# Attention into a token mixer on one core: the third and fourth head group's q and k are transposed in the whole array, and copied out one by one

## The chip, the cores and the metric

The kernel runs on one core of one Trainium2 chip. Its time is the device time in microseconds (us) of one execution; the median of three runs before the change is 184.26 us (183.81 to 184.72). A profile of one execution stands beside these runs. Its engines are TensorE (PE, with its weight loads as PEld), VectorE (DVE), ScalarE (ACT), GpSimd (POOL) and SyncE (SP), whose queue issues most of the transfers.

## The reference

Two steps, in float32, with q, k and v of shape (8 batches, 12 heads, 448 rows, 64 columns):

```
scores = q @ k^T / sqrt(64) - log(448)
x      = sigmoid(scores) @ v             # heads side by side: (8, 448, 768)
W      = (x @ w_q) @ (x @ w_k)^T / sqrt(64)
out    = max(W @ x, 0) @ w_out           # (8, 448, 768)
```

## The kernel before, in words

**The work and its letters.** Four heads of one batch make a head group; there are 24 groups, numbered n = 0 to 23, three to a batch. One letter of the string PLAN (lines 138 to 152) stands for one step, and the loop at line 828 walks through the string once and records the instructions of each step. So PLAN fixes the order of work on every engine; nothing is reordered later. The letters that matter here:

- S: one seventh of a group's scores (`scores`, line 311): four 64x64-tiled matmuls into a pair of PSUM banks, then one sigmoid on ACT over both banks (line 332) into an `at` tile. There are 168 of these, counted from S0. The first seven belong to group 0, S7 to S13 to group 1, S14 to S20 to group 2, and so on.
- P: one seventh of a group's `at @ v` (`values`, line 339): four matmuls into a bank pair that is held for all seven; after the seventh a copy (line 356) takes the result to `xt`.
- q, k (and a, b; and c, d, r, s): bring q or k of a group into the transposed layout `qk` that the scores read (`tr`, line 257). For q and k the transposes are matmuls with an identity, 28 in 64x64 tiles, four of them at a time in the four quarters of the array (`transposes`, line 231). For a and b they are 7 matmuls of 128x128 (`transposes_whole`, line 241). For c, d, r and s POOL and DVE do it without PE.
- 1: the next of the casts that DVE does (the others are POOL's); there are four of them, those marked with a dot in ORDER: q1, v0, k2, v23.
- O: a quarter or half of an output block; D: issue one output store that is ready.

**PSUM.** The eight banks of 2 KB are handed out by hand: each character of BANKS (line 66) is the next answer to "which bank": a digit 0 to 3 names a pair, a letter a to h a single bank (a and b make pair 0, g and h pair 3). A pair or bank that is named again waits for the copy or sigmoid that last read it.

**The four transposes of the change.** Groups 2 and 3 use the letters q and k before. For group 2, q's 28 transposes take pair 0, one S stands between, then k's 28 go into the same pair, and one DVE copy (line 301, 1792 columns) takes both out; the pair is held all the while. Group 3 does the same in pair 3. Which products those are: every matmul and transpose that PE is given has a number, from 0, in the order of the program; the list `products` holds them (3618 before). PE runs them in that order.

**Loads.** q, k and v of a group are float32 loads of 448 KB through SP's queue in the order ORDER (line 703), into a ring of six buffers; a load goes out when the cast of the tile that lay in its buffer is done. POOL casts to bf16 (lines 212 and 222), and rearranges some (lines 167 to 173).

**Two tables of waits on SP.** BEHIND (line 710) says for the last loads at which product they are put into SP's queue and behind which product the transfer has to start: q of group 23 at 2280, behind 2280; v of group 23 at 2816, behind 2530. HELD (line 521) does the same for three output stores of batch 5, behind products 3040, 3168 and 3168. SP is a queue: what stands behind a waiting transfer waits too.

Of the kernel before, what the change touches and what calls it, by code (L numbers as in the profile page):

```python
# [17 lines left out]
def kernel(  # L18
# [29 lines left out]
    def pool(name, bufs, **kw):  # L48
# [15 lines left out]
    pairs = [banks[:, 2 * n : 2 * n + 2] for n in range(4)]  # L64
    pairs16 = [banks16[:, 2 * n : 2 * n + 2] for n in range(4)]
    BANKS = (
        "abcd0123200233111020302312031203101031021g2012020120h1g21320"
        "132123103103213012302g01h20h1g2031a32102312g12h1201321gh0210"
        "12h01210321g201321g2h01gh201g20132cd302c302302131e301230ef31"
        "0ef3102102c302d320d320123cd20gh120g102310g102hg102312gh10210"  # L70
        "ef130210ef1302120120320312321031021021321a310320321320120123"
        "020210320120c3210210312"
    )
    given = list("".join(BANKS))
    held = set()
# [54 lines left out]
    def xt(u, j):  # L130
# [5 lines left out]


    PLAN = (
        "SSFKESSES1EEqESDD1DESjPPppSpDpPDSSSqS1kSpPPSqSpSkSDPPSPSxSxr"
        "sSWwDDDDSSwzDPpSPppSpPSrSwSwWsSPpXSPNpSpPPSUSqSzMSSkpSpPpSMS"  # L140
        "ppPSSxSxMScPpSdPSpppSSPwWwrWSSXWDWSSosOSNPpPSpppzPSSOOSxSrPP"
        "ppSUSsppzPSoSOSoSoSppMpSPPPPSSWOWWWScSdxWODSMDWSOSxCOSMppScP"
# [375 lines left out]

    opened = []
    stores, o_tiles = [], [0]  # L520
    HELD = {(5, 1, 1): 3040, (5, 2, 0): 3168, (5, 2, 1): 3168}

    def flush(n=None):

# [45 lines left out]
    def out_pair(act, tail):  # L570
# [36 lines left out]
        def store():  # L607
            for x in range(2):
                cols = slice(x * NB, (x + 1) * NB)
                if len(us) == 1:  # L610
                    behind_product(
                        (nc.scalar if ends and x else nc.sync).dma_start(
                            out=out[2 * w + us[0]].rearrange("(p i) d -> p i d", i=NI)[:, k : k + 5 : 4, cols], in_=o[HALF[x]],
                        ), HELD.get((2 * w + us[0], k, x), 0),
                    )
# [6 lines left out]

        stores.append((o_tiles[0] - 1, max(HELD.get((2 * w + us[0], k, x), 0) for x in range(2)), store))
        if tail or late:
# [74 lines left out]
    for _ in range(31):  # L699
# [2 lines left out]

    ORDER = (
# [5 lines left out]
    )  # L709
    BEHIND = {("q", 23): (2280, 2280), ("v", 23): (2816, 2530)}  # L710
    BY = {"s": [], "v": []}
    for x in ORDER.split():
        if x[0] == ".":
# [10 lines left out]
    def pump_loads():  # L724
        while len(loaded) < len(ORDER):
            nm, n = ORDER[len(loaded)]
            if len(ring) >= 6 and ring[-6] not in cast:
                break
            emit, m = BEHIND.get((nm, n), (0, 0))
            if emit >= len(products):  # L730
# [204 lines left out]
```

## Time and profile before

| what | value |
|---|---|
| median of three runs | 184.26 us (183.81 to 184.72) |
| the profiled execution's own time | 184.71 us |
| its span, first to last instruction | 182.8 us |
| granted TensorE clock | 0.994 |
| PE busy | 170.4 us (93%) |
| ACT busy | 159.4 us (87%) |
| DVE busy | 134.3 us (73%) |
| POOL busy | 116.8 us (64%) |

The 1.9 us between span and time lie around the program. Busy times are sums over the whole span, and the stages differ: a share says little on what a stage waits for. In the timeline's rows the engine's start and length in us come first, then engine, line, operation and shape; a bracket at the end says how long the engine sat idle before and what ended it. A PE row's length runs to the modelled end of its last matmul, so rows overlap: the distance between starts is what PE took.

### The profile page before, as it was taken

What the parts mean: (1) busy time and instruction counts of PE and PEld (TensorE: products, weight loads), DVE (VectorE), ACT (ScalarE), POOL (GpSimd) and SP (SyncE); (2) the same over time, 40 slices, a digit from 0 to 9 for tenths busy, and PEclk for the clock granted to TensorE, in tenths of its full rate; (3) what the DMA queues carried; (4) which work ended last, traced back from release to release, by engine and by line L of the source; (5) the groups of instructions that cost most, each with busy time, mean ns of one, the idle gap of its engine ahead of it and who ended that gap; (6) DMA issues with size and microseconds to landing.
All of it is one profiled execution on the core that took longest, in us unless ns stands there. A gap on an engine that the chain in (4) does not pass through costs nothing.

```text
span 182.8 us, 8404 instructions
## 1 busy us (share of the span) xinstructions
PE 170.4 (93%) x3617; PEld 112.8 (62%) x3618; DVE 134.3 (73%) x205; ACT 159.4 (87%) x207; POOL 116.8 (64%) x156
## 2 busy tenths in 40 slices
PE   7887789899999999999999999999999999999980
PEld 7644435545564555565556556556788798899960
DVE  2545699988998898988858887689786885694220
ACT  4699999999999999999998999899989979966230
POOL 1336886999589999699999927999999500000000
PEclk9999999999999999999999999999999999999997
DMA  5999999969999677999999999997589343433775
GB/s 174 371 382 274 329 382 398 364 212 279 351 402 331 219 295 207 353 285 349 396 232 327 349 307 292 359 359 250 193 255 252 106 96 87 95 90 93 176 181 164
DMA packets 24261, 48.51 MB, mean 265 GB/s; under 512 B 3872, under 2 KB 16416, under 8 KB 24224
## 3 DMA queue, kind: packets, MB, share of 16 engines
q1 hardware_dynamic: 24000, 47.69, 79.4%
q8 instruction: 28, 0.46, 1.0%
q10 hardware_dynamic: 224, 0.30, 0.7%
q14 instruction: 9, 0.07, 0.1%
HBM read 35.78 MB, written 11.01 MB: 256 GB/s over the span
## 4 chain that ended last, share of the span: by engine, by line
PE 76%; ACT 12%; DMA 3%; POOL 3%; issue 2%; DVE 1%; POOLq 0%; ACTq 0%
PE banks L121 72%; ACT at L332 12%; PE banks L124 4%; DMA ld<-in_v_dram 3%; POOL v L222 1%; POOL qk L212 1%; POOL qk L173 1%; POOL wout L755 0%; DVE xn L385 0%; ACT qk L806 0%; DVE ld L558 0%; ACT ld L558 0%; DVE zeros L691 0%; DVE zeros L690 0%; POOLq L222 0%
## 5 line engine op out<-in xcount | busy, mean ns | idle before, releaser
L332 ACT ACTIVATE at<-banks 128x896 bf16<-128x896 f32 x168 | 141.1, 943 | 5.4 <-PE banks L121 4.8
L121 PE MATMUL banks<-wout,mx 64*64 64x384 bf16 (+2 forms) x816 | 65.4, 324 | 0.0
L121 PE MATMUL banks<-qk 64*64 64x448 bf16 x672 | 60.7, 360 | 3.8 <-ACT at L332 3.0
L212 POOL CAST qk<-ld 128x896 bf16<-128x896 f32 x38 | 44.7, 1191 | 8.2 <-issue 5.6
L121 PEld LDWEIGHTS <-mx 64*64 64x64 bf16 (+2 forms) x816 | 39.2, 105 | 16.2 <-issue 6.0
L121 PE MATMUL banks<-at,v 64*64 64x448 bf16 x672 | 46.5, 350 | 0.8 <-ACT at L332 0.4
L121 PEld LDWEIGHTS <-qk 64*64 64x64 bf16 x672 | 26.5, 105 | 24.8 <-issue 17.8
L356 DVE CAST xt<-banks 128x896 bf16<-128x896 f32 x23 | 25.0, 1086 | 7.6 <-PE banks L121 5.7
L121 PEld LDWEIGHTS <-v 64*64 64x64 bf16 x672 | 22.9, 106 | 6.8 <-issue 1.7
L470 DVE TENSOR_SCALAR mx<-banks 128x896 bf16<-128x896 f32 (+1 forms) x21 | 19.9, 956 | 4.9 <-PE banks L121 4.2
L222 POOL CAST v<-ld 128x896 bf16<-128x896 f32 x22 | 20.3, 930 | 2.9 <-DMA ld<-in_v_dram 2.7
L272 DVE STREAM_TRANSPOSE qk<-qk 128x448 f32<-128x448 f32 x26 | 16.0, 630 | 0.1
L385 DVE COPY xn<-banks 128x896 bf16<-128x896 bf16 x21 | 13.1, 624 | 3.6 <-PE banks L124 2.6
L252 DVE STREAM_TRANSPOSE qk<-qk 32x448 f32<-32x448 f32 x24 | 15.3, 636 | 0.6
L170 POOL COPY qk<-qk 32x448 uint32<-32x448 uint32 x26 | 14.4, 554 | 1.6
L173 POOL COPY qk<-swap 32x448 uint32<-32x448 uint32 x26 | 14.4, 554 | 1.5
L121 PE MATMUL banks<-xt,wqk 64*64 64x448 bf16 (+1 forms) x84 | 13.8, 353 | 0.2 <-ACT at L332 0.2
L651 DVE COPY o<-banks 128x384 f32<-128x384 f32 x17 | 9.4, 554 | 3.4 <-PE banks L121 3.0
L124 PEld LDWEIGHTS <-xt 64*64 64x64 bf16 (+1 forms) x588 | 9.8, 108 | 3.0 <-issue 1.5
L124 PE MATMUL banks<-ident,xt 64*64 64x64 bf16 (+1 forms) x588 | 10.4, 194 | 0.2
L121 PE MATMUL banks<-wqk,tmp 64*64 64x448 bf16 (+3 forms) x72 | 8.5, 291 | 0.0
L121 PE MATMUL banks<-wq,tmp 64*64 64x448 bf16 (+2 forms) x72 | 8.4, 292 | 0.0
(67 smaller groups left out, 135.3 us busy)
## 6 DMA issues: line engine op xcount, KB each, us to landing
ld<-in_q_dram SPq DMA_DIRECT2D x24, 448.0 KB, 6.2
ld<-in_v_dram SPq DMA_DIRECT2D x24, 448.0 KB, 5.9
ld<-in_k_dram SPq DMA_DIRECT2D x23, 448.0 KB, 5.9
out_dram<-o SPq DMA_DIRECT2D x38, 192.0 KB, 4.7
out_dram<-ld SPq DMA_DIRECT2D x14, 192.0 KB, 2.8
ld<-in_moe_w_out_dram SPq DMA_DIRECT2D x6, 384.0 KB, 4.6
wout<-wout SPq DMA_DIRECT2D x6, 192.0 KB, 6.0
out_dram<-o SPq DMA_DIRECT2D x4, 96.0 KB, 1.9
```

The source lines that it names most:

```text
L121: products.append(nc.tensor.matmul(*args, **kw))
L124: products.append(nc.tensor.transpose(*args, **kw))
L170: eng.tensor_copy(out=w[lo, 1], in_=w[hi, 0])
L173: eng.tensor_copy(out=w[hi, 0], in_=z[lo])
L212: COPY[e](out=f[:, :, "qk".index(nm)].rearrange("p e i d y -> p e y i d"), in_=ld.pop((nm, n)).rearrange("p (y i e d) -> p e y i d", y=2, ...
L222: COPY[e](out=t16.rearrange("p i b d -> p b i d"), in_=ld.pop((nm, n)).rearrange("p b (i d) -> p b i d", i=NI),)
L252: nc.vector.transpose(out=qk[n][other : other + 32, h].rearrange("p t i n -> p (t i n)").bitcast(F32), in_=w[own : own + 32, 1 - h],)
L272: nc.vector.transpose(out=qk[n][:, t].rearrange("p t i n -> p (t i n)").bitcast(F32), in_=w)
L332: nc.scalar.activation(dst, src, ACTF.Sigmoid, bias=attn_bias, scale=attn_scale)
L356: COPY[eng](out=xt(u, j), in_=ps)
L385: COPY[eng](out=xn, in_=ps)
L470: nc.vector.tensor_scalar(dst, ps, moe_scale, 0.0, ALU.mult, ALU.max)
```

## The change

The letters of groups 2 and 3 in PLAN become a and b, so each of their four transposes is 7 matmuls of 128x128 into a single bank, with its own DVE copy of 896 columns (line 280) and the bank free after it. In PLAN the letter 1 of k2's cast (the third k) moves from before k2's letter to before q2's. BANKS gets a, b, g and h at these four places in place of pair 0 and pair 3; the pairs of all scores stay as they were. There are 84 products fewer from there on (3534 in all), so a product that had number 2360 has 2276 now.

HELD is emptied: the three stores go when their data is there. In BEHIND, q23 is put into the queue at 2642 (2726 by the old numbers) and starts behind 2276 (2360 by the old numbers); v23 at 2732 (2816), behind 2404 (2488).

```diff
-        "SSFKESSES1EEqESDD1DESjPPppSpDpPDSSSqS1kSpPPSqSpSkSDPPSPSxSxr"
+        "SSFKESSES1EEqESDD1DESjPPppSpDpPDSSS1aSbSpPPSaSpSbSDPPSPSxSxr"
...
-    HELD = {(5, 1, 1): 3040, (5, 2, 0): 3168, (5, 2, 1): 3168}
+    HELD = {}
...
-    BEHIND = {("q", 23): (2280, 2280), ("v", 23): (2816, 2530)}
+    BEHIND = {("q", 23): (2642, 2276), ("v", 23): (2732, 2404)}
```

What now stands in the engines' queues, at three places. On DVE, between the copy of group 0's result (`xt_90`) and that of group 1's (`xt_91`); L222 is the cast of k2, L301 and L280 are the copies out of the banks:

```order
@@ -14,19 +14,19 @@
 L293 COPY qk<-banks 128x2x448
 L356 CAST xt_90<-banks 128x2x7x64
-L222 CAST k_413<-ld_105 128x2x7x64
-L301 COPY qk<-banks 128x2x2x448 x2
+L222 CAST k_380<-ld_105 128x2x7x64
+L280 COPY qk<-banks 128x7x2x64 x4
 L356 CAST xt_91<-banks 128x2x7x64
 L385 COPY xn<-banks 128x896 x2
```

Two copies of both q and k became four of one; the cast (only the number in its name is another) stands where it stood, ahead of the copies and behind `xt_90`.

In SP's queue, at the last load of q (`ld_105`, q of group 23) and the six stores of batch 3 beside it:

```order
@@ -89,6 +89,6 @@
 L198 DMA ld_103<-in_v_dram 128x2x448
 L190 DMA ld_104<-in_k_dram 128x896
+L657 DMA out_dram<-o 64x768 x6
 L190 DMA ld_105<-in_q_dram 128x896
-L657 DMA out_dram<-o 64x768 x6
 L612 DMA out_dram<-o 64x2x384 x2
 L198 DMA ld_100<-in_v_dram 128x2x448
```

The load of q23 went behind the six stores. Nothing else changed its place in SP's queue; the held stores only lost their wait for PE.

A tile's cast is recorded once its load is in the queue (`ready`, line 739), so the cast of q23 is recorded later too. POOL's last work before the change; the first two rows are the casts of k and q of group 23, the next three rearrange both (`arrange`, line 160), and L420 makes the shifted copy of batch 6's `wqk`, once DVE has written that (line 415):

```order
L212 CAST qk_3307<-ld_104 128x2x2x224
L212 CAST qk_3307<-ld_105 128x2x2x224
L167 COPY swap<-qk_3307 128x448
L170 COPY qk_3307<-qk_3307 32x448 x2
L173 COPY qk_3307<-swap 32x448 x2
L420 COPY wq_98<-wqk_96 64x448
```

And after it:

```order
L212 CAST qk_3224<-ld_104 128x2x2x224
L420 COPY wq_98<-wqk_96 64x448
L212 CAST qk_3224<-ld_105 128x2x2x224
L167 COPY swap<-qk_3224 128x448
L170 COPY qk_3224<-qk_3224 32x448 x2
L173 COPY qk_3224<-swap 32x448 x2
```

The cast of q23 and the rearranging moved behind L420. On DVE, the two transposes of group 23 that read the rearranged tile (line 272) stand where they stood, between a store's copy and the copy of group 21's result into `xt`. ACT's queue is the same.

More of the change, by code (lines that the diff above doesn't have):

```diff
@@ L66 @@
     BANKS = (
[L67 to L72, printed above, removed]
+        "abcd0123200233111020302312a3b120g10h1031021g2012020120h1g213"
+        "20132123103103213012302g01h20h1g2031a32102312g12h1201321gh02"
+        "1012h01210321g201321g2h01gh201g20132cd302c302302131e301230ef"
+        "310ef3102102c302d320d320123cd20gh120g102310g102hg102312gh102"
+        "10ef130210ef1302120120320312321031021021321a3103203213201201"
+        "23020210320120c3210210312"
     )
```

8 rows, old and new, of the table ORDER are left out of this document.

## The prediction, made before the change was run

> **What bounds the kernel now.** I read the busy time by stretch first, then the chain of work that ended last, then the timelines of the engines at the places where the change moves something. By stretch (busy us and instructions of PE, PEld, DVE, ACT and POOL, then granted clock, DMA share, GB/s):
>
> ```profile
> 12.00:24.00 12.00, 9.66 (x283) 5.23 (x275) 7.20 (x10) 11.77 (x16) 9.08 (x12) 1.00 0.96 317
> 140.00:160.00 20.00, 20.00 (x542) 17.46 (x537) 14.59 (x21) 18.91 (x24) 4.13 (x7) 1.00 0.43 111
> 160.00:170.00 10.00, 10.00 (x334) 9.44 (x329) 6.45 (x13) 6.31 (x13) 0.00 (x0) 1.00 0.35 88
> ```
>
> Early, ACT is the full engine (11.77 of 12 us) and PE idles 2.3 us. Late, PE never stops, and ACT and DVE have gaps. The chain agrees:
>
> ```profile
> 12.72 0.78 ACT at L332
> 13.53 3.13 ACT at L332 x4
> 16.72 3.08 ACT at L332 x4
> 19.91 0.70 ACT at L332
> ...
> 146.42 12.22 PE banks L121 x292
> ```
>
> The change touches both stages. Early, a sigmoid starts every 0.80 us (S8 at 13.53, S12 at 16.72, S16 at 19.91), and work on PE costs or gains something only if it moves a sigmoid. Late, each us that PE stands still is a us of the total.
>
> **Early: the four transposes.** PE around them, from group 2's q to the scores behind group 3's k:
>
> ```profile
> 14.50 0.46 PE L124 MATMUL banks<-ident,q 64*64 64x64 bf16 x28 [0.43 <-DVE xt L356]
> 14.78 0.38 PE L121 MATMUL banks<-qk 64*64 64x448 bf16 x4
> ...
> 17.73 0.38 PE L121 MATMUL banks<-qk 64*64 64x448 bf16 x4 [0.40 <-ACT at L332]
> ...
> 18.55 0.38 PE L121 MATMUL banks<-qk 64*64 64x448 bf16 x4 [0.24 <-ACT at L332]
> 18.73 0.41 PE L124 MATMUL banks<-ident,k 64*64 64x64 bf16 x28
> 19.36 0.38 PE L121 MATMUL banks<-qk 64*64 64x448 bf16 x4 [0.21 <-ACT at L332]
> ```
>
> The rows with `banks<-qk` are S11, S14, S15 and S16. A tiled group takes 0.28 us (14.50 to 14.78). Seven transposes in the whole array stand later in the trace, between two groups of scores:
>
> ```profile
> 77.44 0.38 PE L121 MATMUL banks<-qk 64*64 64x448 bf16 x4
> 77.75 0.56 PE L124 MATMUL banks<-ident,xt 128*128 128x128 bf16 x7
> 78.25 0.38 PE L121 MATMUL banks<-qk 64*64 64x448 bf16 x4
> ```
>
> They took 0.50 us (77.75 to 78.25) and began 0.31 us after the scores in front, where tiled ones began 0.18 after (18.55 to 18.73). So a whole group costs 0.50 - 0.28 + 0.31 - 0.18 = 0.35 us more, four of them 1.4 us. [...]
>
> I take 0, because PE waits there anyway. q of group 2 starts at 14.50 behind a copy that stays; S11 then starts 0.22 late, at 15.00, and is ready at 15.38, where its sigmoid's turn is 13.53 + 3 x 0.80 = 15.93. The tightest place is k of group 3: it starts at 18.86 and ends at 19.36, just when S16's bank comes free; S16 is ready at 19.74, its turn is 19.91. That is 0.17 us of room. As the other end there is the first whole group of the program:
>
> ```profile
> L124 PE MATMUL banks<-ident,q 128*128 128x128 bf16 x7 | 1.0, 314 | 0.0
> L293 DVE COPY qk<-banks 128x896 bf16<-128x896 bf16 x2 | 1.3, 626 | 1.9 <-PE banks L124 1.9
> 15.52 1.09 DVE L301 COPY qk<-banks 128x1792 bf16<-128x1792 bf16 x1 [0.53 <-PE banks L124]
> ```
>
> At 1.0 us for seven, S16 would be 0.50 - 0.17 = 0.33 us late, and two or three such misses add up to at most 1 us. I stay near 0, since that group came in two pieces behind two casts. On DVE, two copies of 1.09 us become four of about 0.63 (the row of 896 columns): 0.3 us more, on an engine busy 7.2 of 12. Their inputs come at about 15.0 and 15.8, so group 2 is laid out by 16.5, before S14 needs it at 17.73. k2's cast does not move on DVE. The banks that come free sooner help nobody: the scores keep their pairs, and each waits for a sigmoid. Term: 0, from 0 to +1.0.
>
> **Late: q of group 23.** Its load, and how long loads took there (the `ld` tiles from 118 to 150 us):
>
> ```profile
> 129.90 0.33 SPq L190 DMA_DIRECT2D ld<-in_q_dram  x1
> 130.32 5.16 SPq L657 DMA_DIRECT2D out_dram<-o  x6
> 131.72 0.39 PE L124 MATMUL banks<-ident,xt 64*64 64x64 bf16 x28
> DMA to landing us min/median/max: 3.1/4.9/5.6
> ```
>
> It now waits for a transpose that starts at 131.72 (product 2360 by the old numbers) and stands behind six stores of 5.16 us: it goes at 132 to 135.5 and lands by 141. That alone costs nothing, as POOL shows, but POOL's order does:
>
> ```profile
> 138.50 2.31 POOL L212 CAST qk<-ld 128x896 bf16<-128x896 f32 x2
> 142.71 1.17 POOL L173 COPY qk<-swap 32x448 uint32<-32x448 uint32 x2
> 145.68 0.55 POOL L420 COPY wq<-wqk 64x448 bf16<-64x448 bf16 x1 [1.80 <-ACT at L332]
> 144.90 0.62 DVE L415 TENSOR_TENSOR wqk<-banks,wpart 128x448 bf16<-128x448 f32 x1
> 147.97 1.16 DVE L272 STREAM_TRANSPOSE qk<-qk 128x448 f32<-128x448 f32 x2
> 149.05 1.05 DVE L356 CAST xt<-banks 128x896 bf16<-128x896 f32 x1
> ```
>
> Before, q23's cast was the second of the two at 138.50 (from 139.65), and with the rearranging POOL was through at 143.88: 4.23 us of work. Then L420 waited for DVE's L415, which ends at 145.52. Now L420 stands first. It cannot start sooner, so POOL idles from 139.65 to 145.68; L420 ends at 146.23, and q23's 4.23 us end at 150.5.
>
> DVE takes up group 23 at 147.97. It is a queue: now it waits until 150.5, 2.55 us. The two transposes end by 151.6 (1.08 us, as from 147.97 to 149.05), and behind them stands L356, the copy of group 21's result out of bank pair 1, which then runs from 151.6 to 152.7 in place of 149.05 to 150.10.
>
> Who waits for pair 1? PE, as follows:
>
> ```profile
> 148.38 0.41 PE L121 MATMUL banks<-at,v 64*64 64x448 bf16 x4
> ...
> 150.90 0.41 PE L121 MATMUL banks<-qk 64*64 64x448 bf16 x4
> ...
> 152.25 0.80 PE L121 MATMUL banks<-xn,wkn 64*64 64x192 bf16 x28
> 152.83 0.41 PE L121 MATMUL banks<-qk 64*64 64x448 bf16 x4
> ```
>
> The row at 148.38 is the last P of group 21. S157 and S158 take pairs 3 and 2, and S159, at 150.90, is the next to take pair 1. It had 0.8 us to spare. Now it waits until 152.75: PE stands still for 1.85 us, with all that is queued behind S159. That includes what might have filled the gap: PE goes by order. Group 23's first scores (S161, 152.83 before) come 1.2 us behind the end of their transposes even before that delay, so they add nothing. The later copies on DVE had 1.1, 0.9 and 0.9 us idle ahead of them and catch up.
>
> Is any of it made good? PE is busy 20.00 of 20 and 10.00 of 10 us in the two late rows, so it has no slack to give. ACT gets 1.85 us to run ahead, and has nothing to do in it. The only room I see is here:
>
> ```profile
> 147.38 11.82 ACT L332 ACTIVATE at<-banks 128x896 bf16<-128x896 f32 x14 [0.86 <-PE banks L121]
> ```
>
> 11.82 us for fourteen is 0.84 each against a beat of 0.80: nine of them stand behind S159, so if ACT had been the brake there, 0.4 us would come back. Term: +1.85, from +1.4 to +2.4 (the last if POOL, working beside a busy DVE, takes 0.5 us longer).
>
> **Late: v23 and the held stores.** v23 goes some 1 us sooner and is cast much later:
>
> ```profile
> 137.26 0.38 SPq L198 DMA_DIRECT2D ld<-in_v_dram  x1
> 155.40 0.62 DVE L222 CAST v<-ld 128x896 bf16<-128x896 f32 x1
> ```
>
> The freed stores leave a DMA that is busy 43%; nothing behind them in SP's queue had its data. Term: 0.
>
> The sum for the profiled execution: 182.8 + 0 + 1.85 + 0 + 1.9 around the span = 186.55 us. That execution lies 0.45 us above the median of the runs, so for the median: 184.26 + 1.85 = 186.1 us.
>
> **The rivals.** *A: the wait on DVE is absorbed, no change.* It needs PE to find pair 1 free, or slack behind it. For it: only the 0.8 us in hand, already taken off. Against it: three queues in a row, POOL, DVE and PE, each in order. It gives 184.3.
>
> *B: faster.* The place is the beat of ACT: if banks that come free earlier let PE run ahead from 16 us on, the 0.23 us that ACT lacks in 12 to 24 us, and some of PE's waits, could come back, and the late stall would have to be absorbed too. From 1 us it decides: 183.3. Against it: the pairs of the scores are the same.
>
> *C: slower at both ends.* The early term at its +1.0 on top: 187.1.
>
> *D: the clock falls in the stall.* After the last matmul the trace shows what rest does (columns as above):
>
> ```profile
> 177.00:178.00 1.00, 0.58 (x8) 0.15 (x4) 0.41 (x2) 0.32 (x1) 0.00 (x0) 1.00 0.97 238
> 179.00:180.00 1.00, 0.00 (x0) 0.00 (x0) 0.00 (x0) 0.00 (x0) 0.00 (x0) 1.00 1.02 297
> 181.00:182.00 1.00, 0.00 (x0) 0.00 (x0) 0.00 (x0) 0.00 (x0) 0.00 (x0) 0.50 0.07 25
> ```
>
> PE ended at 177.6, and the clock was still whole at 180 and half from 181: a rest of about 3 us. 1.85 is less. [...]
>
> **How the numbers follow.** Forecast 0.76, A 0.11, B 0.04, C 0.05, D 0.04. A measurement of this kernel can tell about 0.5% from no change, 0.9 us: slower is above 185.2. So slower is forecast, C and D: 0.85; same is A, 0.11; faster B, 0.04. The range takes the forecast's term from +1.4 to +2.4, the 0.45 us by which the runs differ, and C: 185.3 to 187.2. A, B and D are outside, 0.19.
>
> **What would show it.** Right: POOL idle from about 139.7 to 145.7 with L420 next; DVE's L272 waiting some 2.5 us for POOL; a PE gap of 1.9 us ahead of S159, with DVE's `xt` named as its end; the early stretch with S16's sigmoid at 19.9. Wrong: PE without idle time between 148 and 155 us (A); S16's sigmoid later than 20.2 (C) or much earlier (B); a clock under 1.00 after 152 us (D).

## The result, and the profile after

| | median | runs | range |
|---|---|---|---|
| the kernel before, measured beside it | 184.5 us | 6 | 183.81 to 185.2 |
| the changed kernel | 186.54 us | 6 | 186.12 to 187.25 |

The changed kernel takes 1.0112 times as long (95% interval 1.0079 to 1.0145): 2.0 us more, where 1.85 us were forecast. Ratios, here and below, leave out the few runs that fell into a slower state of the chip; medians take in all runs. Its profiled execution took 186.12 us, with a span of 184.3 us.

The busy time by stretch of the changed kernel (busy us of PE, PEld, DVE, ACT and POOL, then clock, DMA share, GB/s):

```profile
12.00:24.00 12.00, 10.47 (x199) 5.76 (x191) 7.84 (x12) 11.77 (x16) 8.99 (x12) 1.00 0.94 323
140.00:160.00 20.00, 18.32 (x478) 15.63 (x470) 12.43 (x18) 17.32 (x22) 4.53 (x7) 1.00 0.36 91
160.00:170.00 10.00, 10.00 (x348) 9.08 (x344) 7.85 (x15) 6.81 (x13) 0.00 (x0) 1.00 0.35 82
179.00:180.00 1.00, 0.93 (x12) 0.40 (x8) 0.39 (x2) 0.32 (x1) 0.00 (x0) 1.00 0.96 267
```

Early, PE is busy 0.81 us longer than before (10.47 against 9.66), and ACT, the full engine there, exactly as long: 11.77 us. Late, PE has lost 1.68 of 20 us. In the last row PE ends at 179.9 us, where it ended at 177.6 before: 2.3 us later. The span grew by less, 1.5 us, since in the execution of before that was profiled 5.2 us lay between PE's end and the end of the span, and here 4.4.

The chain of work that ended last, where before one stretch of 12.22 us of PE stood:

```profile
137.36 9.09 PE banks L121 x215
146.89 4.73 PE banks L121 x106
152.25 0.99 DVE xt L356
153.28 7.71 PE banks L121 x186
```

A copy of DVE now stands in the middle of PE's row. The chain names only the last link. To see why that copy ran at 152, one reads the queues backwards: what stood ahead of it on DVE, and what that waited for. These are the rows of POOL, DVE and PE in the timelines:

```profile
138.65 1.20 POOL L212 CAST qk<-ld 128x896 bf16<-128x896 f32 x1
146.15 0.56 POOL L420 COPY wq<-wqk 64x448 bf16<-64x448 bf16 x1 [6.31 <-ACT at L332]
146.77 1.20 POOL L212 CAST qk<-ld 128x896 bf16<-128x896 f32 x1
...
149.88 1.17 POOL L173 COPY qk<-swap 32x448 uint32<-32x448 uint32 x2
145.37 0.62 DVE L415 TENSOR_TENSOR wqk<-banks,wpart 128x448 bf16<-128x448 f32 x1
...
151.08 1.17 DVE L272 STREAM_TRANSPOSE qk<-qk 128x448 f32<-128x448 f32 x2 [2.55 <-POOL qk L173]
152.17 1.05 DVE L356 CAST xt<-banks 128x896 bf16<-128x896 f32 x1
150.88 0.71 PE L121 MATMUL banks<-wout,mx 64*64 64x384 bf16 x12
153.28 0.38 PE L121 MATMUL banks<-qk 64*64 64x448 bf16 x4 [1.68 <-DVE xt L356]
```

POOL stands idle for 6.31 us ahead of L420. Its row names ACT's sigmoid as the releaser, but sigmoids end all the time; what L420 reads is DVE's `wqk` of L415, which ends at 145.99, 0.16 us before L420 starts. Behind L420 stands q23's work, from 146.77 to 151.05. DVE waits 2.55 us for it, L356 runs at 152.17, and PE gets pair 1 at 153.28.

### The profile page after: what moved, and what is told of

It is laid out like the page before. It is cut to its first block, busy times and chain, and to the rows that moved or that the text cites. A ratio compares the mean times of both kernels' runs of the same rounds, so it can differ in the third digit from the quotient of the medians.

```text
span 184.3 us, 8238 instructions
## 1 busy us (share of the span) xinstructions
PE 171.8 (93%) x3533; PEld 113.1 (61%) x3534; DVE 134.7 (73%) x207; ACT 159.6 (87%) x207; POOL 116.9 (63%) x156
## 4 chain that ended last, share of the span: by engine, by line
PE 78%; DVE 8%; ACT 6%; issue 3%; POOL 2%; DMA 2%; SPq 0%; DVEq 0%; ACTq 0%
PE banks L121 73%; ACT at L332 5%; PE banks L124 4%; DVE qk L252 2%; DVE xt L356 2%; DMA ld<-in_moe_w_k_dram 2%; DVE qk L265 1%; DVE mx L470 1%; POOL wqk L759 1%; POOL qk L212 1%; DVE k L222 1%; DVE xn L385 0%; DVE qk L272 0%; DVE wqk L430 0%; ACT qk L806 0%
## 5 line engine op out<-in xcount | busy, mean ns | idle before, releaser
L356 DVE CAST xt<-banks 128x896 bf16<-128x896 f32 x23 | 24.9, 1084 | 7.7 <-PE banks L121 5.8
L470 DVE TENSOR_SCALAR mx<-banks 128x896 bf16<-128x896 f32 (+1 forms) x21 | 19.9, 956 | 5.8 <-PE banks L121 5.1
L222 POOL CAST v<-ld 128x896 bf16<-128x896 f32 x22 | 20.4, 934 | 1.2 <-DMA ld<-in_v_dram 0.9
L272 DVE STREAM_TRANSPOSE qk<-qk 128x448 f32<-128x448 f32 x26 | 16.0, 630 | 2.7 <-POOL qk L173 2.6
```

The source lines that it names most:

```text
L222: COPY[e](out=t16.rearrange("p i b d -> p b i d"), in_=ld.pop((nm, n)).rearrange("p b (i d) -> p b i d", i=NI),)
L272: nc.vector.transpose(out=qk[n][:, t].rearrange("p t i n -> p (t i n)").bitcast(F32), in_=w)
L356: COPY[eng](out=xt(u, j), in_=ps)
L470: nc.vector.tensor_scalar(dst, ps, moe_scale, 0.0, ALU.mult, ALU.max)
```

## The experiments

Two theories stood against each other. The first is that of the prediction: the early transposes cost nothing, and the loss is one chain, from POOL's order over DVE's queue to bank pair 1. The rival puts some or all of it at the early end, or into the late load as such. All ratios are to the kernel before, measured on the same chip between the runs of the experiment.

| experiment | median us | ratio (interval) |
|---|---|---|
| early part alone | 184.38 | 0.9994 (0.9967 to 1.0020) |
| the waits of the last loads alone | 186.84 | 1.0121 (1.0065 to 1.0176) |
| no held stores, alone | 184.87 | 1.0014 (0.9986 to 1.0041) |
| L420 on DVE | 184.38 | 0.9991 (0.9964 to 1.0019) |
| q23 earlier in the queue, load as late | 184.56 | 1.0012 (0.9986 to 1.0039) |
| `xt` ahead of L272 on DVE | 184.42 | 1.0007 (0.9979 to 1.0036) |
| 0.62 us more on POOL | 186.72 | 1.0115 (1.0076 to 1.0153) |
| 1.86 us more on POOL | 189.86 | 1.0255 (1.0200 to 1.0309) |
| transposes twice, changed kernel | 188.24 | 1.0203 (1.0148 to 1.0258) |
| transposes twice, early part alone | 187.56 | 1.0121 (1.0072 to 1.0169) |
| the changed kernel again | 186.28 | 1.0085 (1.0055 to 1.0114) |

**The change in two halves.** First the letters and banks alone, with the old tables in the new numbers (84 lower):

```diff
-    HELD = {}
+    HELD = {(5, 1, 1): 2956, (5, 2, 0): 3084, (5, 2, 1): 3084}
-    BEHIND = {("q", 23): (2642, 2276), ("v", 23): (2732, 2404)}
+    BEHIND = {("q", 23): (2196, 2196), ("v", 23): (2732, 2446)}
```

> The change's early part alone: the four whole-array transposes with their copies, banks and cast, with the two tables of waits as before (their numbers lowered by 84 only). Theory (the late order on POOL carries the whole loss; early PE work lies in waits for ACT): no change, ratio 1.000 within 0.003, POOL's L420 last, no wait of DVE's L272 on POOL, S16's sigmoid at 19.9 us. Rival (early transposes cost the time): slower by 0.5 to 1%, a gap in ACT's row between 15 and 21 us. Rival (the early part gains something that the late loss hides): faster by 0.3% or more.

Twelve runs give 184.38 us against 184.42: no difference. POOL does L420 last again, and PE's timeline has no wait behind 122 us:

```profile
146.84 0.55 POOL L420 COPY wq<-wqk 64x448 bf16<-64x448 bf16 x1 [2.52 <-ACT at L332]
```

Then the kernel before with the waits of the two last loads alone, in its own numbers:

```diff
-    BEHIND = {("q", 23): (2280, 2280), ("v", 23): (2816, 2530)}
+    BEHIND = {("q", 23): (2726, 2360), ("v", 23): (2816, 2488)}
```

> The kernel before, with only the new table of load waits (q23 put into the queue at 2726, behind 2360; v23 behind 2488; the held stores stay held). Theory: POOL's L420 now stands ahead of q23's cast, so the whole loss is here: slower by 1.9 us, ratio 1.010, a PE gap of 1.9 us ahead of S159 ended by the copy of xt. Rival (it takes both parts): ratio under 1.005.

The whole loss is here: 186.84 us. The interval is wide, because three of the six runs lie at 185.7 to 186.0 and three at 187.7 to 188.0; what sets the two groups apart is open, and their mean clocks (0.995 to 1.0 in both) do not tell. The DVE and PE rows show the waits of the changed kernel to 0.01 us:

```profile
150.61 1.17 DVE L272 STREAM_TRANSPOSE qk<-qk 128x448 f32<-128x448 f32 x2 [2.54 <-POOL qk L173]
152.81 0.38 PE L121 MATMUL banks<-qk 64*64 64x448 bf16 x4 [1.67 <-DVE xt L356]
```

The third part, the stores that are no longer held, was made alone in the kernel before.

```diff
-    HELD = {(5, 1, 1): 3040, (5, 2, 0): 3168, (5, 2, 1): 3168}
+    HELD = {}
```

> The kernel before with the three held stores freed and nothing else changed. Theory: no change, ratio 1.000 within 0.003. Rival (the end gains from stores that are out of the way): up to 0.6 us faster, ratio 0.997. Rival (the hold had a use): slower by 0.3% or more.

1.0014 (0.9986 to 1.0041): nothing that can be measured.

**POOL's order, or the late load?** In the changed kernel, batch 6's L420 goes to DVE. The load stays late, and only POOL's queue changes.

```diff
-    (nc.vector if tail else nc.gpsimd).tensor_copy(out=w2[HALF[1], span], in_=w[HALF[0], span])
+    (nc.vector if tail or u == 6 else nc.gpsimd).tensor_copy(out=w2[HALF[1], span], in_=w[HALF[0], span])
```

> The changed kernel with L420 of batch 6 done by DVE (0.3 us there) and not by POOL. q23's load stays as late as in the change and behind the same six stores; only POOL no longer has L420 ahead of the cast. Theory (POOL's order, not the load): q23 is cast at 139 to 140 us, DVE's L272 does not wait for POOL, no PE gap at S159, the time of before within 0.5 us, ratio 0.997 to 1.003. Rival (the late transfer or the stores ahead of it cost the time): the loss of 1.9 us stays, ratio 1.01.

184.38 us: the loss is gone. POOL casts both tiles in one go, L420 costs DVE 0.27 us, and L272 does not wait (it has no bracket):

```profile
138.15 2.30 POOL L212 CAST qk<-ld 128x896 bf16<-128x896 f32 x2
145.54 0.27 DVE L420 COPY wq<-wqk 64x448 bf16<-64x448 bf16 x1
148.06 1.15 DVE L272 STREAM_TRANSPOSE qk<-qk 128x448 f32<-128x448 f32 x2
```

The second way to the same end changes one number: q23 is put into SP's queue 42 products earlier, and its transfer still waits for product 2276.

```diff
-    BEHIND = {("q", 23): (2642, 2276), ("v", 23): (2732, 2404)}
+    BEHIND = {("q", 23): (2600, 2276), ("v", 23): (2732, 2404)}
```

> The changed kernel with one number changed: q23's load is put into SP's queue at product 2600 and not 2642 (it still starts behind product 2276), so its cast is recorded ahead of L420. Theory: the loss is gone, ratio 1.000 within 0.003, POOL's L420 is last again, no PE gap at S159. Rival (the place in POOL's order isn't the cause): 1.01 stays.

That is enough: 184.56 us, 1.0012 (0.9986 to 1.0039). It separates the two best, since the load is no earlier against PE's work. Here is its row in SP's queue, and then that of the changed kernel:

```profile
132.20 0.33 SPq L190 DMA_DIRECT2D ld<-in_q_dram  x1
```

```profile
132.50 0.33 SPq L190 DMA_DIRECT2D ld<-in_q_dram  x1
```

The load goes at 132.20 us, where the kernel that loses 2 us has it at 132.50; PE's products at 125 us are 0.29 us earlier in this execution too. Put into the queue 42 products earlier, its cast is recorded ahead of L420; that is all that differs on POOL, and it is the loss. (In SP's queue the load now stands ahead of four of the six stores; as its time shows, that gains it nothing.) v23's new wait is still in this kernel, so that costs nothing either.

**Is it DVE's queue that hands the delay on?** In the changed kernel, the letters c and d of group 23 are put behind the last P of group 21, so that L356 stands ahead of L272 on DVE. POOL stays as late as it was.

```diff
-        "pPSPoSoMmOSOLScllLSLLSDodODSONxOPSpcpdpDPSPSPoOSoSOSOoSUSoSO"
+        "pPSPoSoMmOSOLScllLSLLSDodODSONxOPSpppDPSPSPcdoOSoSOSOoSUSoSO"
```

> The changed kernel with the two DVE transposes of group 23 put behind group 21's last P, so that on DVE the copy of xt (L356) stands ahead of the two L272. POOL is as late as in the change. Theory (DVE's queue passes the delay on to bank pair 1): POOL idles 6 us as in the change and L272 still waits for it until 150.5 to 151, but L356 runs at 149 to 149.5, PE has no gap at S159, and group 23 is laid out at about 152.2, before S161 at 153: the time of before within 0.6 us, ratio under 1.004. Rival (the late layout of group 23 itself is what PE waits for): the loss stays, now as a gap ahead of S161.

```profile
146.94 0.56 POOL L420 COPY wq<-wqk 64x448 bf16<-64x448 bf16 x1 [6.31 <-ACT at L332]
150.17 1.09 DVE L356 CAST xt<-banks 128x896 bf16<-128x896 f32 x1 [0.85 <-PE banks L121]
151.87 1.17 DVE L272 STREAM_TRANSPOSE qk<-qk 128x448 f32<-128x448 f32 x2 [0.60 <-POOL qk L173]
153.93 0.77 PE L121 MATMUL banks<-xn,wkn 64*64 64x192 bf16 x28 [0.20 <-DVE o L604]
```

POOL idles the same 6.31 us and group 23 is laid out as late as in the changed kernel (L272 starts at 151.87 in an execution that runs 0.79 us later at 125 us), but L356 is through first, and PE's longest wait there is 0.20 us. The time is 184.42 us. So late transposes of group 23 harm nobody; what harms is that they stand ahead of a copy that PE waits for.

**The dose.** In the changed kernel, the first copy of the rearranging (line 167) is issued once more for group 23, 0.62 us of POOL's time.

```diff
+        if n == N - 1:
+            eng.tensor_copy(out=z, in_=w[:, 1])
```

> The changed kernel with 0.62 us more work on POOL in the rearranging of group 23 alone (its first copy into the swap tile is done twice, with the same data). Theory (POOL's lateness goes through DVE to pair 1 one for one): DVE's L272 waits 3.2 us in place of 2.55, the PE gap at S159 is 2.3 us in place of 1.7, and the time is 0.6 us above the changed kernel's, ratio to the kernel before 1.014 (1.012 to 1.017). Rival (some slack takes up lateness on the way): the ratio of the changed kernel, 1.011.

```profile
151.45 1.17 DVE L274 STREAM_TRANSPOSE qk<-qk 128x448 f32<-128x448 f32 x2 [3.17 <-POOL qk L175]
153.65 0.38 PE L121 MATMUL banks<-qk 64*64 64x448 bf16 x4 [2.30 <-DVE xt L358]
```

In the trace both waits are 0.62 us longer than in the changed kernel (3.17 against 2.55, 2.30 against 1.68; the lines are numbered 2 higher). The time, 186.72 us, shows it no better than not: its interval holds the changed kernel's ratio. So a larger dose followed, the same copy three more times, 1.86 us.

```diff
+        if n == N - 1:
+            for _ in range(3):
+                eng.tensor_copy(out=z, in_=w[:, 1])
```

> The changed kernel with the first copy into the swap tile done four times in place of once for group 23 (the same data), 1.86 us more on POOL behind L420. Theory (POOL's lateness reaches the end one for one): DVE's L272 waits 4.4 us, the PE gap at S159 is 3.5 us, and the time lies 1.8 to 1.9 us above the changed kernel's, ratio to the kernel before 1.021. Rival (part of a longer gap is made good behind it, by the clock, ACT or the end): 1.011 to 1.016.

```profile
152.74 1.17 DVE L275 STREAM_TRANSPOSE qk<-qk 128x448 f32<-128x448 f32 x2 [4.44 <-POOL qk L176]
154.94 0.38 PE L121 MATMUL banks<-qk 64*64 64x448 bf16 x4 [3.57 <-DVE xt L359]
```

DVE's and PE's waits grew by 1.89 us each for 1.86 us on POOL: from here each us of POOL is one of PE. The ratio, 1.0255, lies 0.8 us above the 1.021 that was expected. The profiled execution, at 187.77 us, was the fastest of the six, 1.5 us above the changed kernel's 186.28, and was granted a clock of 1.00 in every stretch from 140 to 178 us. The five others took 189.24 to 191.13 us at a mean clock of 0.979 to 0.987, where the changed kernel's runs have 0.991 to 1.0. That fits rival D's mechanism, at a rest of 3.57 us in place of 1.68. The traces bear on it by their ends: the clock fell 3.2 us after PE's last product in the kernel before (177.6 to 180.8) and 4.7 us after it in the changed kernel (179.9 to 184.7), to 0.50 in both. For this kernel's trace I estimate 2.0 to 2.3 us, from its clock of 0.93 and PE's 11.59 busy us between 170 and 186 us, if it fell to 0.50 there too. So a rest of 3.57 us may end before the clock falls or not, and one of 1.68 lies below all three. No trace of such an execution exists, and one run of the kernel before also had 0.985 at 184.85 us, so it is not shown.

**Are the early transposes free, or only cheap?** If PE's waits cover them, twice as many should come out late. In both kernels, each of the 28 matmuls is issued twice, and the tables move by 28.

```diff
-            mt(
-                ps[:, x * P : (x + 1) * P], t16[:, i].rearrange("p b d -> p (b d)"), ident16,
-            )
+            for _ in range(reps):
+                mt(
+                    ps[:, x * P : (x + 1) * P], t16[:, i].rearrange("p b d -> p (b d)"), ident16,
+                )
```

> The changed kernel with each of the four whole-array groups of transposes issued twice over the same bank (14 in place of 7, the table of load waits moved by the 28 products), about 0.45 us more of PE time at each of the four places, 1.8 us in all. Theory (PE's waits for ACT cover 1.4 us of extra work and little more): by the walk through S11 to S16, S12 and S14 miss their sigmoid's turn by 0.3 to 0.4 us each, ACT's row is 0.4 to 1.0 us late at S21, and the time is that much above the changed kernel's, ratio to the kernel before 1.013 to 1.017. Rival (there is more cover): 1.011, ACT's row not late. Rival (no cover, PE work counts in full): 1.021.

> The early part alone (tables of waits as before), with each of the four whole-array groups issued twice: the doubled early work without the late loss. Theory: ACT is 0.7 us late at S14 and at S21, of which part comes back while ACT sets the pace, and the time is 0.3 to 0.8 us above the kernel before, ratio 1.002 to 1.004. Rival (no cover): 1.010. Rival (all covered): 1.000.

ACT's rows of the first of them, from the changed kernel with doubled transposes:

```profile
12.46 6.01 ACT L333 ACTIVATE at<-banks 128x896 bf16<-128x896 f32 x7 [0.24 <-PE banks L121]
18.73 12.28 ACT L333 ACTIVATE at<-banks 128x896 bf16<-128x896 f32 x15 [0.26 <-PE banks L121]
```

The cover can be seen to end: ACT's row, unbroken with single transposes, has a hole ahead of S14. Against the changed kernel's row, moved by the 0.26 us that this execution is ahead at S8, ACT is late by 0.29 us at S12, 0.67 at S14 and 0.73 at S21. That much agrees with the expectation. At S55 it is late by 0.37; whether the rest was made good can't be told from that, since the trace of the early part alone, with single transposes, shifts against the changed kernel by 0.94 us between S21 and S28. The times do not agree: 188.24 us where 1.013 to 1.017 was expected, and 187.56 us where 1.002 to 1.004 was. My expectation of the times fell. In the second of the two kernels PE has three gaps that no semaphore in the profile ends, far behind the edit:

```profile
100.52 0.38 PE L121 MATMUL banks<-qk 64*64 64x448 bf16 x3 [0.41 <-issue]
137.67 0.57 PE L121 MATMUL banks<-at,v 64*64 64x448 bf16 x7 [1.37 <-issue]
169.72 0.84 PE L121 MATMUL banks<-wout,mx 64*64 64x384 bf16 x15 [0.33 <-issue]
```

Together they are 2.11 us of that execution's 187.72; if each reached the end, it would have come to 185.6 without them, which is what was expected. The other doubled kernel has two of 0.23 us, one of them in the same group of matmuls as the 1.37, the kernel without held stores one of 0.52 us at 164.6, and the one with the waits alone one of 0.18 us at 14.7. These seven are all such gaps behind 10 us in the 13 traces, and they have two things in common. Each stands ahead of a product whose number is 95 above a multiple of 128 (1759, 2399 and 3295 in the kernel with the three). And the two near 136 us, the 1.37 and the 0.23 in the same group of matmuls, each end 2.2 to 2.7 us after the half microsecond (135.0 to 135.5 and 133.0 to 133.5) with a transfer of 16 KB in the queue that the page lists under instructions:

```profile
q8 instruction: 28, 0.46, 1.0%
```

It makes 28 transfers in a run of 3562 products, about one for every 128. My guess from these numbers is that PE waits there for its own next instructions, and that 28 products more move the places where it can; no run shows it. One execution of each doubled kernel was traced, so their medians say nothing on what the early transposes cost.

**Again.** The changed kernel was run once more, as it is, in more runs.

> The changed kernel itself once more, as the measure for the two beside it on the same chip. Expected: ratio to the kernel before 1.011 within 0.003, the PE gap ahead of S159 again 1.7 us.

186.28 us against 184.85 for the kernel before, 1.0085 (1.0055 to 1.0114): 1.4 us more by the medians, where the first measurement had 2.0. Both intervals hold 1.010, which is 1.85 us. In the trace PE waits 1.69 us ahead of S159, as expected.

## Why the prediction was right, point by point

**Early: right, the term is 0.** The rows that the walk spoke of, in the changed kernel's PE timeline:

```profile
14.50 0.55 PE L124 MATMUL banks<-ident,q 128*128 128x128 bf16 x7 [0.43 <-DVE xt L356]
14.98 0.38 PE L121 MATMUL banks<-qk 64*64 64x448 bf16 x4
...
18.54 0.38 PE L121 MATMUL banks<-qk 64*64 64x448 bf16 x4 [0.24 <-ACT at L332]
18.86 0.56 PE L124 MATMUL banks<-ident,k 128*128 128x128 bf16 x7
19.35 0.38 PE L121 MATMUL banks<-qk 64*64 64x448 bf16 x4
```

S11 was walked to 15.00 us and started at 14.98; k of group 3 was walked from 18.86 to 19.36 and took 18.86 to 19.35. The whole groups of the trace at 77 us were the right price: 0.48 and 0.49 us here. The dearer end, 1.0 us for seven as in the program's first group, did not come. S16 is the second of the two sigmoids in this row of ACT, and starts at 19.91 as before:

```profile
19.11 1.81 ACT L332 ACTIVATE at<-banks 128x896 bf16<-128x896 f32 x2
```

PE paid both parts of the price, but in its waits for ACT: the four groups took 0.20 us more each (0.48 in place of 0.28), which is the 0.81 us of extra busy time, and the seam is the 0.32 us from 18.54 to 18.86, where tiled transposes came 0.18 after the scores. On the path, both parts together would have been the 1.4 us.

**DVE's copies: right in the sum, not in a part.** Group 2 was to be laid out by 16.5 us; the two copies ended at 16.76, because k2's cast, which "does not move", took 1.12 us in this execution in place of 0.63 (below). S14 needs them at 17.73, so it cost nothing.

**Late: right, link by link.** Up to here the execution runs 0.47 us behind that of before; with that added, the steps are those forecast. The load of q23 was to go at 132 to 135.5 us: 132.50. POOL's idle time was to last from 139.65 to 145.68: 139.85 to 146.15. DVE's wait was put at 2.55 us and is 2.55. L356 was to run at 151.6: 152.17. S159 was to come at 152.75: 153.28. Matched product by product, PE was 0.47 us behind the execution of before ahead of S159 and 2.38 at it: the stall is 1.91 us, where 1.85 was the term, and the other end, 2.4, was not needed: q23's 4.23 us on POOL took 4.28 (146.77 to 151.05), and no run shows the 0.5 us more beside a busy DVE. (The 1.68 us in PE's bracket are idle time alone. They begin at the modelled end of the matmuls in front, 0.23 us after the moment at which S159 would have started without a wait.)

**Late, v23 and the held stores: right, 0.** The kernel with q23 earlier in the queue has v23's new wait and no held stores, and lies at 1.0012; the freed stores alone came to 1.0014.

**Made good: nothing, as put.** PE's last products start 2.35 us late, against 2.38 at S159. The 0.4 us that ACT might have given back did not come.

**The step with a wrong size: between the two places.** The sum had nothing there. In fact 0.47 us of the lateness is collected ahead of the stall, 0.13 us in the first 118 us and 0.34 us near 120. A DVE copy comes late there. Its row follows, with the last matmuls that it waits for, first before, then in the changed kernel:

```profile
118.86 0.26 PE L121 MATMUL banks<-wq,tmp 64*64 64x224 bf16 x2
119.26 1.09 DVE L470 TENSOR_SCALAR mx<-banks 128x896 bf16<-128x896 f32 x1 [0.24 <-PE banks L121]
```

```profile
118.99 0.26 PE L121 MATMUL banks<-wq,tmp 64*64 64x224 bf16 x2
119.77 1.09 DVE L470 TENSOR_SCALAR mx<-banks 128x896 bf16<-128x896 f32 x1 [0.61 <-PE banks L121]
```

DVE is idle 0.37 us longer. The bracket names PE, but that wait is over: the matmuls end at 119.12 before and at 119.25 here, and L470 follows them by 0.14 us before and by 0.52 here. PE's next scores start as L470 ends, at 120.91 us, another 0.31 us late. The step is the same in two more traces with the early part (the early part alone and q23 earlier in the queue, idle for 0.62 us each), and it is missing in that of the freed stores alone, which lacks the early part (0.24 us). The order of work and the waits are the same there; L470 is now DVE's 192nd instruction in the trace, where it was its 190th, for the two more copies. What DVE does in that time is open. In the median it can't be told: the early part alone came to 0.9994.

**The sum.** 186.55 us were worked out for the profiled execution, and it took 186.12: 0.06 us more in the stall and 0.47 ahead of it, less 0.85 us by which this execution's end came sooner behind PE's, and 0.1 in small terms. That these misses have opposite signs is luck; the stall itself is not. For the median 186.1 was said, and it is 186.54; 0.24 us of that is the kernel before, which came to 184.5 beside it in place of 184.26.

**The rivals.** A (absorbed) would have needed PE to go on through 152 us; it has its gap there. B (faster) fell with the early part at 0.9994. C (slower at both ends) fell with it too. D (the clock) did not come at this length of rest: 1.00 in all stretches from 140 to 170 us. Its 3 us of rest were read from one trace, where they are 3.2; in the changed kernel's they are 4.7, and 1.68 is less than both. Its place above the range rests on 3 us of PE's work at half clock, which no run shows: in these two traces the clock is at 0.50 only behind PE's last product, before for 4.2 us (180.8 to 184.9).

## What to carry to other kernels

A load's place in its own queue can also set the place of the work that consumes it on another engine, and that second order may be what counts: with the load going out at 132 us either way, one place on POOL made 2 us. When an in-order engine gets a wait, list what stands behind it on that engine, and look there for the copy that frees a bank or a buffer for the full engine; the delay of the waiting work itself (group 23's transposes) can be harmless. The cure is then a choice of three single steps, each of which brought all of it back: order on POOL, another engine for the blocking copy, or order on DVE; none of them came out faster than the kernel before.

## What the runs showed of the hardware

Two casts from SBUF to SBUF, k's on DVE and v's on POOL, hold each other up in these runs where they overlap. In these two timelines they fall together; first the changed kernel, then the one with q23 earlier in the queue:

```profile
14.36 1.12 DVE L222 CAST k<-ld 128x896 bf16<-128x896 f32 x1
14.06 0.94 POOL L222 CAST v<-ld 128x896 bf16<-128x896 f32 x1 [0.16 <-DMA ld<-in_v_dram]
```

```profile
13.97 0.62 DVE L222 CAST k<-ld 128x896 bf16<-128x896 f32 x1
14.11 1.28 POOL L222 CAST v<-ld 128x896 bf16<-128x896 f32 x1 [0.22 <-DMA ld<-in_v_dram]
```

Whichever starts first takes its full speed (0.94 us on POOL, 0.62 on DVE), and the other is longer by what was left of the first, less about 0.14 us: 1.12 for 0.62 with 0.64 us left, 1.28 for 0.94 with 0.48 left. In eight of the ten traces read for this the two casts overlap by 0.14 us or more, and all eight fit that within 0.02 us; in the two others (the freed stores alone and the changed kernel again, which overlap by 0.04 us and not at all) each takes its full speed. Which one starts first differs from execution to execution, as the load lands. The prediction took k2's cast at its duration alone; here that cost nothing, since the copies behind it had 1 us in hand.
